# Retention: where the key-value products of a head pair are formed, summed and read

## The chip, the cores and the metric

The kernel runs on one core of a Trainium2 chip. The metric is the device time of one execution in microseconds. The engines are named as the profile names them: PE is TensorE (PEld its weight loads), DVE is VectorE, ACT is ScalarE, POOL is GpSimd, SP is SyncE, whose queue issues nearly all transfers.

## What is computed

Three stages follow each other, all in float32. First comes retention for 8 batches, 8 heads, 576 tokens and a head size of 64: causal attention without a softmax, where each score is damped by a power of the head's decay.

```python
scores = scale * np.matmul(q, k.transpose(0, 1, 3, 2))
gamma = 1.0 - 2.0 ** (-5.0 - np.arange(H, dtype=np.float32))
Dmat = np.where(rel >= 0, gamma[:, None, None] ** rel[None, :, :], 0.0)
return np.matmul(scores * Dmat[None], v)
```

Its output, 4608 tokens of 512 features, goes through `h = x @ w_in; (h * cos(h)) @ w_out` with 2048 hidden features, and that through a maximum of three projections to 768 features and a last product. The change is in the first stage.

## The kernel before

**Retention in chunks.** The 4608 tokens are taken in 9 blocks of 512 (`NB`). Sequences are 576 long, so most blocks hold the end of one sequence and the start of the next. `chunks_of` cuts a block at the sequence boundary and then into chunks of at most 128 tokens; blocks 1, 3, 5 and 7 get two chunks of 64. The token columns of a block are put in an order with the full chunks first and the two short ones together in the last 128 columns (`column_tokens`), and the host undoes that order at the end.

A unit of work is one block and one pair of heads (36 units, `att_unit`). Its load (`att_load`, line 560) brings query and key by feature, and key and value by token, 8,192 bytes per partition. GpSimd multiplies the values by the growth `gamma ** -pos`, a column of constants per unit (`att_scale`, 566). TensorE forms the scores of each chunk (`att_scores`, 578), VectorE masks them into SBUF (`att_mask`, 587). Each pair of heads has a running state of keys times values, 128x128 in a PSUM bank `state` that all pairs share and hold throughout; only the two diagonal 64x64 squares of it, one per head, are used. Chunk by chunk, ScalarE copies the state to SBUF for the chunk's later use and clears it where a sequence ends (`att_keep`, 605 and 607), and TensorE adds the chunk's product to it (`att_state`, 621). Then TensorE forms the outputs: each chunk's own part from the masked scores (`att_out`, 637, a head in each half of the array's columns) and the part from the kept state (649, two heads in opposite quarters). VectorE multiplies the result by the decay, chunk by chunk (`att_decay`, 664), into the input of the projections.

**The projections** use seven products of half-sized matrices in place of eight, each in three passes of a high and a low part of the operands. VectorE and GpSimd form the differences (386), ScalarE the high parts (390), VectorE the low parts (394). TensorE's products of the first projection during attention are line 417; line 439 is the later form for two blocks at a time. ScalarE and VectorE move sums out of PSUM (464, 470, 487), and `gate` computes `h * cos(h)` (521 to 534). Beside this, `background` prepares later weights: ScalarE widens (186, 187), VectorE joins (191, 192), GpSimd totals (198).

**What sets the order.** The kernel writes the order of every engine out by hand. `at(n, fn, turn)` puts work `n` slots ahead on an agenda with four turns, and `tick` at the end of a slot runs it. A slot after the lead is one product of the projections. Turn `INSIDE` is run in the middle of a slot's product, `AHEAD` at its end, `AFTER` and `LATER` behind that:

```python
at(start, lambda: att_scores(n), AHEAD)
for i in range(5):
    at(start + i + 1, lambda i=i: att_state(n, i), INSIDE)
at(start + 5, lambda: att_out(n), AHEAD)
at(start + 6, lambda: att_decay(n))
```

The first 8 units start 2 slots apart in a lead of 17 slots without projections, the others 3.75 slots apart on average (`start_of`). Each engine works through its queue in that order. PSUM has eight banks, given out in the order of the program (`bank`); SBUF tiles for units and weights come from a pool of eight (`w14`), for the rest from a pool of 25 (`x4`).

## Time and profile before

| | |
|---|---|
| Median of three runs | 1413.91 us (1413.03 to 1415.06) |
| Span of the profiled execution | 1410.5 us |
| Time of that execution outside its span | not recorded |
| PE busy | 1386.8 us, 98%, 8476 matmuls |
| DVE busy | 1130.2 us, 80% |
| ACT busy | 811.5 us, 58% |
| POOL busy | 189.6 us, 13% |

The profile is of one execution. "Busy" is time in which an engine has an instruction under way; a busy PE may still be waiting inside a pipeline. A group of instructions is named by its line, its engine, its output and its inputs. An idle time is put down to what ended it. The chain of waits follows the last instruction back, step by step, to what released it; a piece of the chain is the time for which that instruction held up what came after. An fp32 product is two passes (two records) on PE.

### The profile page before, as it was taken

Reading aid. Unit: us, or ns where it says so; the run is one execution under the profiler, and the core shown is the slowest. Engines: PE = TensorE matmul, PEld = TensorE weight load, DVE = VectorE, ACT = ScalarE, POOL = GpSimd, SP = SyncE. Lnnn points to the kernel's source line nnn. Section 1 sums busy time; section 2 is a strip of 40 time slices with the busy share of each in tenths; the row PEclk is TensorE's granted clock in tenths of the full one; section 3 lists DMA queues with packets and bytes.
Section 4 is the critical chain, followed back from the end, with each engine's and each line's share of the span. In section 5 each row is a group of like instructions: output and inputs, shape, how many; then the busy total and the mean of one; then the engine's idle time right before and its main releaser. Section 6 shows DMA issues by size and latency. Waiting matters only on the chain.

```text
span 1410.5 us, 22294 instructions
## 1 busy us (share of the span) xinstructions
PE 1386.8 (98%) x8476; PEld 1191.2 (84%) x8476; DVE 1130.2 (80%) x1532; ACT 811.5 (58%) x1322; POOL 189.6 (13%) x148
## 2 busy tenths in 40 slices
PE   7999999999999999999999999999999999999998
PEld 5899999998888887788888888889888888888887
DVE  7978888789677879989879999578678567868885
ACT  4566666567687676766546566444454344544543
POOL 3334443341011100000011110110010000000000
PEclk8999999999999999999999999999999999999999
DMA  9689988887989986475578987434434486345633
GB/s 367 236 291 315 312 313 308 293 323 253 412 307 376 337 292 239 185 269 194 175 247 228 296 238 224 124 125 167 172 112 142 147 323 234 102 157 165 230 105 119
DMA packets 112938, 333.36 MB, mean 236 GB/s; under 512 B 9920, under 2 KB 18112, under 8 KB 107200
## 3 DMA queue, kind: packets, MB, share of 16 engines
q1 hardware_dynamic: 109952, 322.51, 63.8%
q0 software_dynamic: 2880, 9.44, 3.8%
q8 instruction: 66, 1.08, 0.3%
q14 instruction: 40, 0.33, 0.1%
HBM read 194.02 MB, written 137.89 MB: 235 GB/s over the span
## 4 chain that ended last, share of the span: by engine, by line
PE 78%; DVE 4%; DMA 4%; ACT 1%; issue 1%; SPq 0%; POOL 0%; DVEq 0%; ACTq 0%
PE d_e L439 13%; PE d_g L928 11%; PE in L439 9%; PE b_e L439 6%; PE b_g L928 6%; PE d_a L417 5%; PE d_u L1458 5%; PE a_e L439 3%; PE a_g L928 3%; PE b_u L1458 2%; PE b_a L417 2%; PE d_b L417 2%; PE sc L578 1%; PE sums L417 1%; PE po L637 1%; PE a_u L1458 1%
## 5 line engine op out<-in xcount | busy, mean ns | idle before, releaser
L928 PE MATMUL d_g<-h_g,w_wo 128*128 128x512 f32 x512 | 157.9, 390 | 0.5 <-ACT o_g L951 0.5
L439 PE MATMUL in<-y,w_wi 128*128 128x512 f32 x672 | 153.6, 390 | 0.7 <-ACT s_a L1064 0.7
L439 PEld LDWEIGHTS in<-y,w_wi 128*128 128x128 f32 x672 | 125.8, 188 | 27.9 <-ACT s_a L1064 2.0
L895 DVE TENSOR_TENSOR l_g<-q_g,h_g 128x1024 fp32r<-128x1024 f32 x96 | 116.7, 1228 | 12.9 <-ACT h_g L888 9.3
L464 ACT ACTIVATE ext<-d_e 128x512 f32<-128x512 f32 x72 | 43.1, 599 | 144.9 <-PE d_e L439 144.9
L417 PE MATMUL d_a<-x_x,w_wi 128*128 128x256 f32 x864 | 122.8, 291 | 0.2 <-DVE x_x L394 0.2
L888 ACT CAST h_g<-q_g 128x1024 fp32r<-128x1024 f32 x96 | 98.9, 1051 | 32.2 <-DVE q_g L879 22.0
L417 PEld LDWEIGHTS d_a<-x_x,w_wi 128*128 128x128 f32 x864 | 109.0, 192 | 5.8 <-issue 1.7
L928 PEld LDWEIGHTS d_g<-h_g,w_wo 128*128 128x128 f32 x512 | 95.8, 188 | 20.6 <-ACT o_g L951 0.9
L928 PE MATMUL d_g<-l_g,w_wo 128*128 128x512 f32 x256 | 99.9, 390 | 0.2 <-DVE l_g L895 0.2
L525 DVE SCALAR_TENSOR_TENSOR t_a<-s_a,t_a 128x1024 f32<-128x1024 f32 x68 | 87.8, 1291 | 14.6 <-ACT t_a L521 13.8
L534 DVE SCALAR_TENSOR_TENSOR s_a<-t_a,s_a 128x1024 f32<-128x1024 f32 x68 | 89.9, 1322 | 10.0 <-ACT t_a L531 10.0
L605 ACT COPY u<-state 128x128 f32<-128x128 f32 x128 | 31.5, 266 | 94.7 <-PE state L621 94.2
L521 ACT ACTIVATE t_a<-s_a 128x1024 int32<-128x1024 f32 x68 | 72.0, 1059 | 21.6 <-DVE s_a L1067 15.3
L439 PE MATMUL d_e<-h_e,w_b 128*128 128x512 f32 x304 | 81.4, 390 | 0.1
L531 ACT ACTIVATE t_a<-t_a 128x1024 f32<-128x1024 f32 x68 | 72.0, 1058 | 13.6 <-DVE t_a L525 13.5
L928 PE MATMUL b_g<-h_g,w_wo 128*128 128x512 f32 x256 | 79.2, 390 | 0.4 <-ACT h_g L888 0.3
L468 DVE TENSOR_TENSOR ext<-ext,b_e 128x512 f32<-128x512 f32 x36 | 24.7, 686 | 59.7 <-PE b_e L439 52.0
L439 PEld LDWEIGHTS d_e<-h_e,w_b 128*128 128x128 f32 x304 | 56.9, 188 | 12.2 <-DVE ext L468 0.5
L417 PE MATMUL b_a<-x_x,w_wi 128*128 128x256 f32 x432 | 61.2, 289 | 1.2 <-DVE u L587 1.2
L566 POOL TENSOR_TENSOR u<-u,cs 128x512 f32<-128x512 f32 x36 | 46.5, 1294 | 81.4 <-DMA u<-att 72.1
L928 PEld LDWEIGHTS d_g<-l_g,w_wo 128*128 128x128 f32 x256 | 48.0, 188 | 11.0 <-DVE l_g L895 1.0
(367 smaller groups left out, 3373.7 us busy)
## 6 DMA issues: line engine op xcount, KB each, us to landing
u<-att SPq DMA_DIRECT2D x36, 1024.0 KB, 7.4
gqp<-s_a SPq DMA_DIRECT2D x64, 512.0 KB, 6.4
q_g<-gqp SPq DMA_DIRECT2D x64, 512.0 KB, 7.0
xsp<-x_x SPq DMA_DIRECT2D x56, 512.0 KB, 6.3
y<-xsp SPq DMA_DIRECT2D x56, 512.0 KB, 8.3
mqp<-ext SPq DMA_DIRECT2D x24, 512.0 KB, 3.6
st_b<-p_b SPq DMA_DIRECT2D x21, 512.0 KB, 6.4
w_b<-st_b SPq DMA_DIRECT2D x5, 1792.0 KB, 12.0
```

Source lines behind the costliest of these rows:

```text
L417: nc.tensor.matmul(h[:, p * HB : (p + 1) * HB], a, b, start=first and p == 0 and i == 0, stop=i == len(terms) - 1, skip_group_check=True,)
L439: nc.tensor.matmul(dst, a, b, start=first and i == 0, stop=i == len(terms) - 1, skip_group_check=True)
L464: nc.scalar.activation(dst, b[:, :n], AF.Copy, scale=scale)
L521: nc.scalar.activation(st["t"], s, AF.Copy, bias=0.25)
L525: nc.vector.scalar_tensor_tensor(out=r, in0=s, scalar=MOST_TURNS, in1=st["t"], op0=ALU.min, op1=ALU.subtract)
L531: nc.scalar.activation(r, r, AF.Sin, scale=TURN, bias=HALF_PI)
L534: nc.vector.scalar_tensor_tensor(out=s, in0=f32(st["t"]), scalar=-1.0, in1=s, op0=ALU.max, op1=ALU.mult)
L566: nc.gpsimd.tensor_tensor(out=v, in0=v, in1=cs[:, col : col + 8].unsqueeze(2).to_broadcast([128, 8, 64]), op=ALU.mult)
L888: nc.scalar.copy(h, ts[i][q])
L895: nc.vector.tensor_tensor(out=lo, in0=t, in1=f32(h), op=ALU.subtract)
L928: nc.tensor.matmul(to, a, v[:, p].rearrange("p (b n) -> p b n", b=2) if half and n == 2 else v[:, :, r], start=first and k == 0 and p == 0 ...
L1458: nc.tensor.matmul(dst, a, v, start=first and p == 0 and i == 0 and (wide or mt == 0), stop=p == 2 and i == 2, skip_group_check=True,)
```

## The change

The state bank, the copies of it and its clears go. Instead, each unit's keys times values are formed for each chunk and head by itself, 64x64, in a PSUM bank of their own, the two heads in the two halves of the array's columns (`att_products`). That is done in one go, right ahead of the outputs of the unit before (`att_visit`). ScalarE copies a unit's products out in one instruction, and GpSimd adds them up from chunk to chunk in SBUF (`att_states`); what crosses a block lies in `carry`, two places per pair in a tile that is not used otherwise at that time. Where a chunk of 64 ends a sequence, GpSimd clears its key rows, so that the product over all 128 rows is that of the other short chunk alone.

Queries and outputs keep their natural token order: the score product of two short chunks takes its query columns in two runs, the outputs of the short chunks are products of their own, and the decays are applied to 256 columns at a time, cut only where a sequence begins. The growth factors come with each unit's load, eight columns, and no longer with the constants, whose decay tables are 256 wide. The grouping of the rest of the kernel is not touched.

```diff
@@ -63,11 +63,11 @@
 CG = 0
-CM = CG + NPAIR * CH
+CM = CG + NPAIR * HB
 CM2 = CM + CH
 CGS = CM2 + CH
-CTV = CGS + NPAIR * 9
-NCONST = CTV + NBLK * NPAIR * 8
+NCONST = CGS + NPAIR * 9
+NTV = 8
 def constants():
@@ -76,18 +76,23 @@
     p = np.arange(128)
     for hp in range(NPAIR):
         g = gamma[2 * hp + p // 64]
-        c[:, CG + hp * CH : CG + (hp + 1) * CH] = g[:, None] ** np.arange(CH) / math.sqrt(D) / WSCALE
+        c[:, CG + hp * HB : CG + (hp + 1) * HB] = g[:, None] ** np.arange(HB) / math.sqrt(D) / WSCALE
         c[:, CGS + hp * 9 : CGS + (hp + 1) * 9] = g[:, None] ** (64 * np.arange(9))
     c[:, CM : CM + CH] = np.arange(CH)[None, :] >= p[:, None]
     c[:, CM2 : CM2 + CH] = c[:, CM : CM + CH] * ((np.arange(CH) // 64)[None, :] == (p // 64)[:, None])
+    return c.astype(np.float32)
+def growths():
+    gamma = (1.0 - 2.0 ** (-5.0 - np.arange(H, dtype=np.float32))).astype(np.float64)
+    tv = np.zeros((NBLK, NPAIR, 128, NB // CH, 2), np.float64)
     for j in range(NBLK):
-        pos = (column_tokens(j) % S).reshape(NB // CH, CH)
+        pos = (column_tokens(j) % S).reshape(NB // CH, CH).astype(np.float64)
         for hp in range(NPAIR):
-            for s in range(4):
-                for e in range(2):
-                    col = CTV + ((j * NPAIR + hp) * 4 + s) * 2 + e
-                    c[:, col] = gamma[2 * hp + e] ** (-pos[s].astype(np.float64))
-    return c.astype(np.float32)
+            for e in range(2):
+                tv[j, hp, :, :, e] = gamma[2 * hp + e] ** -pos.T
+    return tv.reshape(NBLK, NPAIR, 128, NTV).astype(np.float32)
@@ -553,29 +558,40 @@
         units[n] = {
             "qk": w[:, : 2 * NB].rearrange("p (a n) -> p a n", a=2),
             "kv": w[:, 2 * NB : 4 * NB].rearrange("p (a n) -> p a n", a=2),
-            "ret": w[:, 4 * NB : 6 * NB].rearrange("p (a n) -> p a n", a=2),
-            "um": w[:, 6 * NB :].rearrange("p (k n) -> p k n", n=CH),
-            "kept": {},
+            "tv": w[:, 4 * NB : 4 * NB + NTV],
+            "ret": w[:, 4 * NB + NTV : 6 * NB + NTV].rearrange("p (a n) -> p a n", a=2),
+            "sums": w[:, 6 * NB + NTV : 6 * NB + NTV + 4 * D].rearrange("p (k n) -> p k n", n=D),
+            "w": w,
         }
-        nc.sync.dma_start(out=w[:, : 4 * NB], in_=att[j, hp])
+        nc.sync.dma_start(out=w[:, : 4 * NB + NTV], in_=att[j, hp])
     def att_scale(n):
-        v = units[n]["kv"][:, 1].rearrange("p (s d) -> p s d", d=64)
-        col = CTV + n * 8
-        nc.gpsimd.tensor_tensor(
-            out=v, in0=v, in1=cs[:, col : col + 8].unsqueeze(2).to_broadcast([128, 8, 64]), op=ALU.mult
-        )
+        u = units[n]
+        v = u["kv"][:, 1].rearrange("p (s d) -> p s d", d=64)
+        nc.gpsimd.tensor_tensor(out=v, in0=v, in1=u["tv"].unsqueeze(2).to_broadcast([128, 8, 64]), op=ALU.mult)
+        for _, m, c, pos in chunks_of(order_of(n)[0]):
+            if m < CH and pos + m == S:
+                s, p = divmod(c, CH)
+                nc.gpsimd.memset(u["kv"][p : p + m, 0, s * CH : (s + 1) * CH], 0.0)
     def att_scores(n):
         u = units[n]
-        qT, kT = u["qk"][:, 0], u["qk"][:, 1]
+        ch = chunks_of(order_of(n)[0])
         u["sc"] = [bank(f"sc{n}_{e}") for e in range(2)]
         for s in range(NB // CH):
             sl = slice(s * CH, (s + 1) * CH)
+            runs = sorted((c, a) for a, _, c, _ in ch if c // CH == s)
             for e in range(2):
                 r = slice(64 * e, 64 * e + 64)
-                nc.tensor.matmul(u["sc"][e][:, sl], kT[r, sl], qT[r, sl], start=True, stop=True)
+                a = runs[0][1]
+                if len(runs) == 1:
+                    q = u["w"][r, a : a + CH]
+                else:
+                    apart = runs[1][1] - a
+                    q = u["w"][r, a : a + 2 * apart].rearrange("p (b d) -> p b d", b=2)[:, :, : CH // 2]
+                nc.tensor.matmul(u["sc"][e][:, sl], u["qk"][r, 1, sl], q, start=True, stop=True)
     def att_mask(n):
         u = units[n]
@@ -591,63 +607,71 @@
                         op=ALU.mult,
                     )
-    def att_keep(n, i):
...
+    def grown(n):
+        ch = chunks_of(order_of(n)[0])
+        return [i for i, (_, m, _, pos) in enumerate(ch) if pos + m < S]
+    def att_products(n):
+        u = units[n]
+        ch = chunks_of(order_of(n)[0])
+        kn, v = u["kv"][:, 0], u["kv"][:, 1]
+        u["kv_sums"] = b = bank(f"kv{n}")
+        for k, i in enumerate(grown(n)):
+            s = ch[i][2] // CH
+            for e in range(2):
+                cols = slice(s * CH + 64 * e, s * CH + 64 * e + 64)
+                nc.tensor.matmul(
+                    b[64 * e : 64 * e + 64, k * D : (k + 1) * D], kn[:, cols], v[:, cols], start=True, stop=True
+                )
+    def att_states(n):
         u = units[n]
         j, hp = order_of(n)
         ch = chunks_of(j)
-        if i >= len(ch):
-            return
-        _, m, _, pos = ch[i]
-        st = state[:, hp * CH : (hp + 1) * CH]
-        if pos:
-            um = u["kept"][i] = u["um"][:, len(u["kept"])]
-            nc.scalar.copy(um, st)
-        if pos + m == S:
-            nc.scalar.activation(st, cs[:, CM : CM + CH], AF.Copy, scale=0.0)
-    def att_state(n, i):
...
+        of = grown(n)
+        su = u["sums"]
+        nc.scalar.copy(su[:, : len(of)], u["kv_sums"][:, : len(of) * D].rearrange("p (k n) -> p k n", n=D))
+        before = carry[hp][(j + 1) % 2]
+        u["state"] = {}
+        for i, (_, m, _, pos) in enumerate(ch):
+            if pos:
+                u["state"][i] = before
+            if i not in of:
+                continue
+            k = of.index(i)
+            dst = carry[hp][j % 2] if i == len(ch) - 1 else su[:, k]
+            if pos:
+                nc.gpsimd.tensor_tensor(out=dst, in0=before, in1=su[:, k], op=ALU.add)
+            elif i == len(ch) - 1:
+                nc.gpsimd.tensor_copy(dst, su[:, k])
+            before = dst
+    def att_out(n):
         u = units[n]
         j, hp = order_of(n)
         ch = chunks_of(j)
-        if i >= len(ch):
-            return
-        kn, v = u["kv"][:, 0], u["kv"][:, 1]
-        _, m, c, pos = ch[i]
-        if pos + m < S:
-            s, p = divmod(c, CH)
-            sl = slice(s * CH, (s + 1) * CH)
-            nc.tensor.matmul(
-                state[:, hp * CH : (hp + 1) * CH],
-                kn[p : p + m, sl],
-                v[p : p + m, sl],
-                start=False,
-                stop=True,
-                skip_group_check=True,
-            )
-    def att_out(n):
...
         qT, v = u["qk"][:, 0], u["kv"][:, 1]
         po = u["po"] = bank(f"po{n}")
-        for s in range(NB // CH):
+        for i, (a, m, c, _) in enumerate(ch):
+            s = c // CH
             for e in range(2):
                 nc.tensor.matmul(
-                    po[64 * e : 64 * e + 64, s * CH : (s + 1) * CH],
+                    po[64 * e : 64 * e + 64, a : a + m],
                     v[:, s * CH + 64 * e : s * CH + 64 * e + 64],
-                    u["ret"][:, e, s * CH : (s + 1) * CH],
-                    start=s == 0,
+                    u["ret"][:, e, c : c + m],
+                    start=i == 0,
                     stop=False,
                     skip_group_check=True,
                 )
-        for i, um in u["kept"].items():
-            _, m, c, _ = chunks_of(j)[i]
+        for i, st in u["state"].items():
+            a, m, _, _ = ch[i]
             for e in range(2):
                 r = slice(64 * e, 64 * e + 64)
                 nc.tensor.matmul(
-                    po[r, c : c + m], um[r, r], qT[r, c : c + m], start=False, stop=True, skip_group_check=True
+                    po[r, a : a + m], st[r], qT[r, a : a + m], start=False, stop=True, skip_group_check=True
                 )
     def att_decay(n):
@@ -657,39 +681,44 @@
         half = f"k{hp // 2 + 1}"
         if half not in o:
             o[half] = x4(f"{half}_x{j}", [2, NB])
-        for _, m, c, pos in chunks_of(j):
-            t, cc = divmod(c, HB)
-            g = CGS + hp * 9 + pos // 64
+        cuts = sorted({0, HB, NB, (-j * NB) % S} & set(range(NB + 1)))
+        for lo, hi in zip(cuts, cuts[1:]):
+            t, cc = divmod(lo, HB)
+            g = CGS + hp * 9 + (j * NB + lo) % S // 64
             at_ = (hp % 2) * HB + cc
             nc.vector.scalar_tensor_tensor(
-                out=o[half][:, t, at_ : at_ + m],
-                in0=u["po"][:, c : c + m],
+                out=o[half][:, t, at_ : at_ + hi - lo],
+                in0=u["po"][:, lo:hi],
                 scalar=cs[:, g : g + 1],
-                in1=cs[:, CG + hp * CH : CG + hp * CH + m],
+                in1=cs[:, CG + hp * HB : CG + hp * HB + hi - lo],
                 op0=ALU.mult,
                 op1=ALU.mult,
             )
+    def att_visit(n):
+        if n + 1 < NUNIT:
+            att_products(n + 1)
+        att_out(n)
     def att_unit(n, start):
         at(max(0, start - 1), lambda: att_scale(n))
         at(start, lambda: att_scores(n), AHEAD)
-        at(start, lambda: att_keep(n, 0), AFTER)
         at(start + 1, lambda: att_mask(n))
-        for i in range(5):
-            at(start + i + 1, lambda i=i: att_state(n, i), INSIDE)
-            if i < 4:
-                at(start + i + 1, lambda i=i: att_keep(n, i + 1), AFTER)
-        at(start + 5, lambda: att_out(n), AHEAD)
+        if not n:
+            at(start + 1, lambda: att_products(n), AHEAD)
+            at(start + 1, lambda: att_states(n))
+        at(start + 5, lambda: att_visit(n), AHEAD)
+        if n + 1 < NUNIT:
+            at(start + 5, lambda: att_states(n + 1))
         at(start + 6, lambda: att_decay(n))
     NUNIT = NBLK * NPAIR
     nc.sync.dma_start(out=cs, in_=cst)
-    state = bank("state")
-    nc.tensor.matmul(state, cs[:, :CH], cs[:, :NB], start=True, stop=True, skip_group_check=True)
-    nc.vector.memset(state, 0.0)
+    carry = [[f32(spare)[:, (2 * hp + k) * D : (2 * hp + k + 1) * D] for k in range(2)] for hp in range(NPAIR)]
     sums_bank = bank("sums")
     nc.tensor.matmul(sums_bank, cs[:, :CH], cs[:, :NB], start=True, stop=True, skip_group_check=True)
     lead = {}
@@ -1568,9 +1597,7 @@
...
+        "att": np.concatenate([by_feature(q, slice(None)), by_feature(k, idx), by_token(k), by_token(v), growths()], axis=3),
```

The lines left out are the bodies of the old `att_keep`, `att_state` and `att_out`, which stand above, and the host's reordering.

## Rows read from the trace of the kernel before

**Rows 1.** Busy time by stretch: us; PE, PEld, DVE, ACT, POOL busy (instructions); PEclk, DMA share, GB/s.
```profile
20.00:66.30 46.30, 44.33 (x514) 37.97 (x513) 46.02 (x107) 26.90 (x71) 15.71 (x14) 0.99 0.74 265
66.30:320.00 253.70, 253.16 (x2562) 232.40 (x2561) 207.17 (x358) 160.50 (x321) 101.05 (x68) 1.00 0.87 308
320.00:338.40 18.40, 15.87 (x147) 15.20 (x146) 18.11 (x28) 11.83 (x21) 4.19 (x3) 1.00 0.48 174
```

**Rows 2.** Waits of PE, 44 to 330 us: us in total, times, longest.
```profile
PE b_a L417 <- DVE u L587: 1.2, 1, 1.2
PE state L621 <- ACT state L607: 0.8, 1, 0.8
```

**Rows 3.** Timeline of DVE and PEld near 62 us: start us, us, instruction.
```profile
62.30 0.69 DVE L394 TENSOR_TENSOR x_x<-tb_x,x_x 128x512 fp32r<-128x512 f32 x1
...
62.60 1.51 PEld L417 LDWEIGHTS d_a<-x_x,w_wi 128*128 128x128 f32 x12
```

**Rows 4.** The chain of waits after attention: start us, us, what.
```profile
361.76 122.44 PE in L439 x540
```

**Rows 5.** State products in the chain; lines 621 and 637, 66 to 330 us (durations ns).
```profile
286.84 0.41 PE state L621 x2
...
298.10 0.22 PE state L621 x2
...
L621 PEld LDWEIGHTS state<-u x184: 182/192/192, 67.7 to 321.7; 128*128 128x128 f32 x160, 64*128 64x128 f32 x24
...
L637 PEld LDWEIGHTS po<-u x432: 132/137/137, 72.5 to 325.6; 128*64 128x64 f32 x144
```

**Rows 6.** Output products in the chain: start us, us, passes.
```profile
171.79 0.80 PE po L649 x12
...
182.32 0.81 PE po L649 x16
...
289.29 0.92 PE po L649 x16
...
306.60 1.02 PE po L637 x16
307.63 1.02 PE po L649 x16
```

**Rows 7.** DVE reading PSUM: one timeline row; groups, 44 to 320 us (busy us, mean ns).
```profile
328.11 1.12 DVE L664 SCALAR_TENSOR_TENSOR k_x<-po,cs 128x128 f32<-128x128 f32 x4
...
L664 DVE SCALAR_TENSOR_TENSOR k_x<-po,cs 128x128 f32<-128x128 f32 x104 | 30.0, 340 | 6.7 <-PE po L649 6.6
...
L470 DVE SCALAR_TENSOR_TENSOR s_a<-b_a,s_a 128x512 f32<-128x512 f32 x15 | 10.3, 690 | 20.2 <-PE b_a L417 20.2
```

**Rows 8.** Timeline of POOL: a clear and a subtraction.
```profile
0.24 0.10 POOL L1582 MEMSET const-float32-0.0<- 128x1 f32 x1 [0.24 <-issue]
...
220.77 1.27 POOL L386 TENSOR_TENSOR tb_x<-k_x,ta_x 128x512 f32<-128x512 f32 x1
```

**Rows 9.** Timeline of DVE and POOL at 329 to 332 us.
```profile
329.15 0.41 DVE L205 TENSOR_TENSOR s_wi<-fa_wi 128x256 f32<-128x256 f32 x1
...
330.69 1.47 POOL L386 TENSOR_TENSOR ta_x<-k_x,k_x 128x512 f32<-128x512 f32 x1
...
330.93 1.51 DVE L207 TENSOR_TENSOR s_wi<-fa_wi 128x256 f32<-128x256 f32 x1
```

**Rows 10.** Timeline of PE at 164.7 us.
```profile
164.71 1.22 PE L417 MATMUL d_a<-x_x,w_wi 128*128 128x256 f32 x8 [0.25 <-DVE x_x L394]
```

**Rows 11.** Groups of ACT: busy us, mean ns, idle before and its releaser.
```profile
L605 ACT COPY u<-state 128x128 f32<-128x128 f32 x128 | 31.5, 266 | 94.7 <-PE state L621 94.2
...
L219 ACT ACTIVATE w_wi<-fa_wi 128x256 fp32r<-128x256 f32 x2 | 0.8, 417 | 0.3 <-POOL fa_wi L198 0.3
```

**Rows 12.** DMA issues: count, KB each, median us to landing.
```profile
u<-att SPq DMA_DIRECT2D x36, 1024.0 KB, 7.4
...
w_b<-st_b SPq DMA_DIRECT2D x5, 1792.0 KB, 12.0
```

More of the change, by code (lines that the diff above doesn't have):

```diff
@@ L613, in att_state @@
         ch = chunks_of(j)
-        if i >= len(ch):
-            return
-        kn, v = u["kv"][:, 0], u["kv"][:, 1]
-        _, m, c, pos = ch[i]
-        if pos + m < S:
-            s, p = divmod(c, CH)
-            sl = slice(s * CH, (s + 1) * CH)
-            nc.tensor.matmul(
-                state[:, hp * CH : (hp + 1) * CH],
-                kn[p : p + m, sl],
-                v[p : p + m, sl],
-                start=False,
-                stop=True,
-                skip_group_check=True,
-            )
-    def att_out(n):
-        u = units[n]
-        j, hp = order_of(n)
         qT, v = u["qk"][:, 0], u["kv"][:, 1]
         po = u["po"] = bank(f"po{n}")
-        for s in range(NB // CH):
+        for i, (a, m, c, _) in enumerate(ch):
+            s = c // CH
             for e in range(2):
                 nc.tensor.matmul(
-                    po[64 * e : 64 * e + 64, s * CH : (s + 1) * CH],
+                    po[64 * e : 64 * e + 64, a : a + m],
                     v[:, s * CH + 64 * e : s * CH + 64 * e + 64],
-                    u["ret"][:, e, s * CH : (s + 1) * CH],
-                    start=s == 0,
+                    u["ret"][:, e, c : c + m],
+                    start=i == 0,
                     stop=False,
@@ L1556, with by_feature @@
     idx = np.concatenate([column_tokens(j) for j in range(NBLK)])
-    def by_feature(a):
-        a = a.transpose(1, 3, 0, 2).reshape(NPAIR, 128, T)[:, :, idx]
+    def by_feature(a, order):
+        a = a.transpose(1, 3, 0, 2).reshape(NPAIR, 128, T)[:, :, order]
         return a.reshape(NPAIR, 128, NBLK, NB).transpose(2, 0, 1, 3)
@@ L1570 @@
     arrays = {
-        "att": np.stack([by_feature(q), by_feature(k), by_token(k), by_token(v)], axis=3).reshape(
-            NBLK, NPAIR, 128, 4 * NB
-        ),
+        "att": np.concatenate([by_feature(q, slice(None)), by_feature(k, idx), by_token(k), by_token(v), growths()], axis=3),
         "w_in": by_column(moe_w_in),
@@ L1593 @@
     got = got.reshape(NBLK, 128, 2, 2, 2, HB).transpose(0, 3, 5, 2, 4, 1).reshape(T, DM)
-    back = np.empty(T, np.int64)
-    back[idx] = np.arange(T)
-    return np.ascontiguousarray(got[back])
+    return np.ascontiguousarray(got)
```

## The prediction

> **What bounds the kernel now.** The page's busy table puts TensorE at 98% of the span. That is an average, so the view that I read next is busy time by stretch. Attention fills the first 326 us, and its stretches differ [rows 1]: from 20 to 66.3 us VectorE is busy 46.02 of 46.30 us; from 66.3 to 320 us TensorE 253.16 of 253.70 and VectorE 207.17; to 338.4 us VectorE again 18.11 of 18.40. The reader should see a TensorE that never stops between 66.3 and 320 us, with a VectorE that has 46.5 us to spare; before and after, VectorE sets the pace. The waits of TensorE say the same: from 44 to 330 us the two longest kinds are 1.2 and 0.8 us in all [rows 2]. Late in the early stretch TensorE is only a hair behind VectorE: the product whose weight loads start at 62.60 us takes a low operand that is being made from 62.30 to 62.99 us, and reads it from its fifth load of twelve on, some 0.5 us after the first [rows 3].
>
> From 362 us on nothing of the change is touched, and there the chain runs through TensorE for 122 us at a stretch [rows 4]. I let that part move as a block.
>
> **TensorE, the term that carries the forecast.** In the chain a state product of a full chunk costs 0.22 us, one of a 64-row chunk 0.41 us [rows 5]. After 66 us there are 184 records of line 621, two to an fp32 product: 92 products, of which 12 have 64 rows. They cost 80 x 0.22 + 12 x 0.41 = 22.5 us. The last two, up to 321.7 us, lie where VectorE is about to lead; without their 0.44 us, 22.1 us are on the path.
>
> The new products come in pairs, one per head, each 64 columns wide in output and in moving data, in two column halves. No row shows that form, so I price it from the carried-state outputs of line 649, whose two heads lie in opposite quarters of the array [rows 6]. A unit with three 128-token chunks (12 passes) takes 0.80 us, one with four (16 passes) 1.02: 0.055 us per pass. A unit with eight passes of 128 columns and eight of 64 takes 0.81: so eight passes of 64 cost what four of 128 do, plus 0.01, which is 0.029 each. A unit with twelve and four should then take 0.80 + 4 x 0.029 = 0.92, and does. The outputs of line 637, with all 128 rows and column halves as in the new products, also take 1.02 for 16 passes, so full rows are no dearer. Products for units 10 to 35 fall after 66 us: 90 chunks (3 in each of units 10 and 11, then 4, 3, 4, 3, 4, 3 in four units each), 360 passes. At 0.029 that is 10.4 us. The bounds are nothing (hidden in idle halves) and 0.055 us, the pass of 128 columns: 19.8 us. I take 0.029, since the 64-column pass is the nearest form. Net: 10.4 - 22.1 = **-11.7 us**.
>
> The other edits to TensorE are free. In the four blocks with 64-token chunks the outputs are split, eight passes of 64 columns for four of 128: +0.01 us a unit by the price above. Products and outputs share one visit and the column halves, so no change of array form is added to the one that line 637 enters now. The query columns in two runs have as many elements as before. State products of unit n+1 stand ahead of the outputs of unit n in TensorE's queue already, so the products bring these no new wait for a load.
>
> **VectorE.** The decay of a unit was four or five instructions and is now two or three. Four of 128 columns run in 1.12 us [rows 7]; each is 0.340 us long, so the next starts 0.26 after the last. Of 256 columns none is shown; between 0.340 (128) and 0.690 (512) a straight line gives 0.457. Two take 0.38 + 0.46 = 0.83, so 0.29 us a unit go; where the cuts leave three, 0.15 to 0.29: about 9 us over 36 units. That counts only where VectorE leads: seven units before 62 us (-2.0 us) and two after 320 us (**-0.6 us**). The middle has slack already.
>
> **GpSimd, and what it costs VectorE.** New there are 96 additions and 8 copies of 128x64 and 16 clears of 64x128. The nearest rows are a subtraction of 128x512 at 1.27 us and a clear of one column at 0.10 [rows 8]. One eighth of the difference, plus 0.10: an estimate of 0.25 us, bounds 0.10 and 1.27. GpSimd has room, at 101 of 253.7 us [rows 1]. But VectorE pays: a 128x256 addition takes 0.41 us alone and a subtraction of the same size 1.51 while GpSimd subtracts for 1.47 beside it [rows 9]. About half of VectorE's time goes to forms with both inputs in SBUF, so I charge half of 0.25 us per addition. Early: 24 additions, +3.0 us, less the 2.0 of the decays: **+1.0 us**, and TensorE's own saving is worth nothing there because VectorE leads. Bounds: -2.0 (no collision) and +4.0 (each one in full). Middle: 80 operations x 0.125 = 10 us more, less 6.5 by decays; VectorE goes from 207.2 to 211 us in a stretch of 242. It stays second, but at single points it delivers with nothing over, as at 164.71 us, where TensorE waits 0.25 us for a low operand [rows 10]. TensorE now comes to each such point some 0.5 us sooner. I charge three of seven blocks 0.5 us: **+1.5 us**, bounds 0 and 3.5.
>
> Here the rows and the Trainium skill meet. Its page "SBUF — State Buffer", section "Who interferes with whom", says that VectorE with two SBUF inputs and GpSimd reading SBUF shut each other out for a whole instruction. The 1.51 against 0.41 us agrees with a full block. By that rule each early addition would cost 0.25 and not 0.125 us, and the sum would be 3 us higher.
>
> **ScalarE.** 128 copies of 0.266 us go, and the 32 clears beside them; 36 copies of up to 128x256 come, at 0.417 by the nearest row [rows 11]. That frees over 19 us of an engine at 160 of 254 us and is worth nothing by itself. It waited 94 us for state products, but TensorE hardly waited for it [rows 2]. The new copy waits for the products of its visit, with that slot's evictions queued behind: one wait of the old kind where four were. The additions wait for the copy, and behind them on GpSimd stand the next unit's scaling and the weight totals. The sums are read at the next visit, 9.7 us later (27 visits between 72.5 and 325.6 us [rows 5]), and copy and three additions take 1.2 us; the cover is gone only if GpSimd is 8 us late.
>
> **DMA and the start.** The growth factors move from the constants to each load: 32 bytes more on 8,192 per partition, 0.4% of 7.4 us. Rows of 14,336 bytes take 12.0 us, less than in proportion, so a longer row costs nothing more [rows 12]. No DMA is added or moved on a queue. The constants grow by 224 columns, 115 KB at the early 265 GB/s [rows 1]: **+0.4 us** before everything else, bounds 0 and that. The state bank's clearing product goes, off the path, as the first scores wait for data anyway. PSUM: one bank was held by the state throughout; now each unit's products hold one for a moment. A visit wants two banks, for products and outputs, eight in use at most, as before.
>
> **Sum.** -11.7 - 0.6 + 1.0 + 1.5 + 0.4 = -9.4 us on a span of 1410.5. Of the profiled execution the span alone is given; the median of three runs, 1413.0 to 1415.1, is 3.4 us above it. Off the median: 1413.9 - 9.4 = **1404.5 us**. A change of 0.2%, 2.8 us, is about what a measurement here can tell from none.
>
> **Rivals.**
> *The early stretch gives too.* If the additions slip between VectorE's operations, the decays' 2.0 us stay and the 1.5 us are not lost: -11.7 - 0.6 - 2.0 + 0.4 = -13.9, 1400 us, and less with some of TensorE's early saving. For it: GpSimd is idle two thirds of the early stretch. Against: VectorE is not. Chance 0.15.
> *VectorE takes half.* Its 20.2 us of waits for TensorE before line 470 [rows 7] show that TensorE feeds it and it catches up in bursts. If every block's burst is tight, half of the 11.7 us is lost: 1410 us. Chance 0.13.
> *Slower, through GpSimd's additions.* Place: VectorE. Price: the whole addition. If one takes 0.5 us and every one collides, the early stretch grows by 24 x 0.5 - 2.0 = 10 us; in the middle VectorE rises by 40 - 6.5 to 241 us, level with TensorE's 242, and I count 4 us of waits there: -11.7 - 0.6 + 10 + 0.4 + 4 = +2.1, and more where the level load is uneven: 1417 us. It decides from about 0.45 us per addition. For it: the fixed cost of an addition is not shown. Against: 1.27 us for eight times the elements [rows 8]. Chance 0.08.
> *The halves do not overlap.* If the new pairs run one after the other, a pass costs 0.055 us: -2.3 in place of -11.7, in all 0.0: 1413.9 us, no change. Against: line 637's pairs. Chance 0.07.
>
> The forecast has 0.57, with a range of its own of 1399 to 1409. Faster: 0.56 of it, 0.15, and 0.09 of the half case: 0.80. Same: 0.01 + 0.03 + 0.06 = 0.10. Slower: 0.08 + 0.01 + 0.01 = 0.10. The range 1397 to 1412 leaves out the slower case, that of no change and the edges.
>
> **What would show it.** Right: passes of the products near 0.03 us in the chain, no wait of TensorE for a state copy, additions of about 0.25 us, line 664 (whatever its new number) under 0.9 us a unit, the second projection group still starting near 66 us, attention ending some 10 us sooner. Wrong: TensorE waiting for GpSimd's sums or VectorE's low operands by several us, additions of 0.5 us, product passes of 0.05.

## The result, and the profile after

The changed kernel takes 1398.5 us (median of four, 1397.2 to 1401.0) beside 1414.5 us for the kernel before on the same chip: a ratio of 0.9886, interval 0.9872 to 0.9901. The forecast was 1404.5 us, so the sign and the side were right, the time lies inside the range, and the gain was 16 us where 9.4 were forecast. The profiled execution of the changed kernel took 1398.66 us, its span 1396.9; the span before was 1410.5, so 13.6 us went inside the span, and it is these that the steps below account for. The medians are 2.4 us further apart than the spans: the median stands 4.0 us above the span of before's profiled execution, and 1.6 above that of the changed kernel's.

The page's head of the changed kernel (busy us, share of the span, instructions):

```profile
span 1396.9 us, 22865 instructions
...
PE 1365.9 (98%) x8794; PEld 1177.2 (84%) x8794; DVE 1127.0 (81%) x1467; ACT 789.8 (57%) x1198; POOL 234.2 (17%) x268
```

TensorE issues 318 matmul records more than before and is busy 21 us less. The same view by stretch as [rows 1], cut at the places that answer to 66.3, 320 and 338.4 us:

```profile
20.00:66.38 46.38, 41.18 (x603) 36.00 (x599) 46.10 (x88) 21.02 (x42) 28.60 (x41) 0.98 0.74 279
66.38:306.84 240.46, 239.76 (x2792) 222.55 (x2791) 206.18 (x318) 145.45 (x232) 131.91 (x158) 1.00 0.89 324
306.84:325.00 18.16, 15.69 (x144) 15.01 (x144) 18.11 (x26) 10.81 (x19) 4.30 (x3) 1.00 0.48 175
```

The pattern is the old one: VectorE full, TensorE full, VectorE full. Only the middle has shrunk. GpSimd went from 101 to 132 us there, VectorE from 207 to 206.

To compare kernels I use three marks. **A** is the start of the second group of projections; between A and **B** TensorE leads; B is the end of the last product in the chain of waits before VectorE takes over (in every run the same product); **C** is the start of the first product after TensorE's one long wait.

| kernel | median, us | ratio to before | A | A to B | B to C | span |
|---|---|---|---|---|---|---|
| before | 1414.5 | 1 | 66.30 | 253.9 | 18.1 | 1410.5 |
| changed | 1398.5 | 0.9886 (0.9872 to 0.9901) | 66.38 | 240.5 | 17.7 | 1396.9 |

From C to the end it is 1072.1 us before and 1072.4 after. So the change took 13.4 us out of the middle, 0.5 out of the tail, and put 0.1 on the start.

The chain of waits of the changed kernel (start us, us, what and how many passes), two visits that answer to [rows 5] and [rows 6]:

```profile
265.84 0.62 PE kv L625 x16
266.45 0.89 PE po L661 x20
267.34 0.92 PE po L673 x16
...
283.56 1.44 PE b_a L422 x12
285.00 0.50 PE kv L625 x12
285.50 0.88 PE po L661 x16
286.37 1.02 PE po L673 x16
287.39 3.06 PE d_a L422 x24
```

Products (line 625) and the outputs behind them (661) take 0.50 + 0.88 = 1.38 us for 12 product passes and 0.62 + 0.89 = 1.51 for 16; the outputs alone took 1.02 before. That is 0.030 us a pass; 0.029 was forecast.

The groups of the new instructions, 0 to 330 us (busy us, mean ns, then idle time before and its releaser), and for the first group of line 647 also its shortest, median and longest in ns:

```profile
L689 DVE SCALAR_TENSOR_TENSOR k_x<-po,cs 128x256 f32<-128x256 f32 (+3 forms) x96 | 34.2, 406 | 4.6 <-PE po L673 4.6
...
L647 POOL TENSOR_TENSOR u<-u 128x64 f32<-128x64 f32 x48 | 24.0, 501 | 15.6 <-ACT u L636 13.1
...
L647 POOL TENSOR_TENSOR u<-spare,u 128x64 f32<-128x64 f32 x24 | 11.2, 466 | 73.4 <-ACT u L636 73.4
...
L647 POOL TENSOR_TENSOR spare<-u 128x64 f32<-128x64 f32 x24 | 10.3, 427 | 1.3
...
L576 POOL MEMSET u<- 64x128 f32 x16 | 3.2, 198 | 0.0
L649 POOL COPY spare<-u 128x64 f32<-128x64 f32 x8 | 1.9, 236 | 0.0
```

```profile
L647 POOL TENSOR_TENSOR u<-u x48: 316/322/1342, 12.0 to 304.5; 128x64 f32<-128x64 f32 x48
```

The median addition takes 0.32 us, not 0.25, and single ones of that group up to 1.34; the mean over all 96 is 0.47. TensorE's waits in the middle (total us, times, longest), first of the kernel before, 66 to 320 us, then of the changed kernel, 66 to 305 us, come to 0.5 us in both, so the forecast hand-overs added nothing:

```profile
PE state L621 <- ACT u L605: 0.3, 1, 0.3
PE d_a L417 <- DVE x_x L394: 0.2, 1, 0.2
```

```profile
PE d_a L422 <- DVE x_x L399: 0.3, 1, 0.3
PE po L661 <- DVE k_x L689: 0.2, 1, 0.2
```

### The profile page after: what moved, and what is told of

It reads as the page before. It is cut to its first block, busy times and chain, and to the rows that moved or that the text cites. A ratio compares the mean times of both kernels' runs of the same rounds, so it can differ in the third digit from the quotient of the medians.

```text
span 1396.9 us, 22865 instructions
## 1 busy us (share of the span) xinstructions
PE 1365.9 (98%) x8794; PEld 1177.2 (84%) x8794; DVE 1127.0 (81%) x1467; ACT 789.8 (57%) x1198; POOL 234.2 (17%) x268
## 4 chain that ended last, share of the span: by engine, by line
PE 70%; DVE 5%; DMA 4%; ACT 1%; issue 1%; SPq 0%; POOL 0%; DVEq 0%; ACTq 0%
PE d_e L444 13%; PE d_g L957 11%; PE in L444 9%; PE b_e L444 6%; PE b_g L957 6%; PE d_u L1487 5%; PE a_e L444 3%; PE a_g L957 3%; PE b_u L1487 2%; PE d_a L422 2%; PE d_b L422 2%; PE a_u L1487 1%; PE b_b L422 1%; PE b_a L422 1%; DMA gqp<-s_a 1%
## 5 line engine op out<-in xcount | busy, mean ns | idle before, releaser
L422 PE MATMUL d_a<-x_x,w_wi 128*128 128x256 f32 x864 | 117.8, 289 | 1.3 <-DVE u L603 0.7
L957 PEld LDWEIGHTS b_g<-h_g,w_wo 128*128 128x128 f32 x256 | 47.9, 188 | 11.3 <-ACT h_g L917 1.6
L957 PEld LDWEIGHTS d_g<-l_g,w_wo 128*128 128x128 f32 x256 | 48.1, 188 | 10.8 <-DVE l_g L924 1.0
L422 PEld LDWEIGHTS b_a<-x_x,w_wi 128*128 128x128 f32 x432 | 54.1, 191 | 2.1 <-issue 0.3
```

What stands on the lines that cost most here:

```text
L422: nc.tensor.matmul(h[:, p * HB : (p + 1) * HB], a, b, start=first and p == 0 and i == 0, stop=i == len(terms) - 1, skip_group_check=True,)
L957: nc.tensor.matmul(to, a, v[:, p].rearrange("p (b n) -> p b n", b=2) if half and n == 2 else v[:, :, r], start=first and k == 0 and p == 0 ...
```

## The experiments

Ratios are to the kernel before on the same chip. Where the same kernel was run again, A, A to B and B to C repeated within 0.1, 0.5 and 0.1 us; what comes after C differed by several us from execution to execution (1072.4 and 1075.3). So causes are read from the marks, and the whole time only says whether it holds. B to C is left blank where no wait of 2 us or more by TensorE follows B, or where that wait stands elsewhere.

| kernel | median, us | ratio (interval) | A | A to B | B to C | span |
|---|---|---|---|---|---|---|
| no_adds | 1399.7 | 0.9895 (0.9882 to 0.9909) | 64.69 | 241.2 | 17.6 | 1398.8 |
| full_rows | 1407.9 | 0.9962 (0.9949 to 0.9975) | 68.09 | 250.1 | 18.1 | 1408.6 |
| full_width | 1407.7 | 0.9955 (0.9942 to 0.9968) | 67.36 | 249.9 | 17.7 | 1405.9 |
| decay_128 | 1400.9 | 0.9904 (0.9888 to 0.9919) | 67.15 | 241.6 | 18.1 | 1401.4 |
| after_again | 1400.9 | 0.9912 (0.9898 to 0.9926) | 66.44 | 240.9 | 17.6 | 1400.3 |
| adds_x3 | 1423.9 | 1.0079 (1.0066 to 1.0091) | 75.9 | 254.6 | | 1421.1 |
| apart | 1410.0 | 0.9979 (0.9970 to 0.9987) | 67.34 | 249.6 | | 1407.9 |
| late_split | 1396.8 | 0.9884 (0.9871 to 0.9898) | 66.48 | 240.7 | | 1394.1 |
| adds_dve | 1431.0 | 1.0129 (1.0106 to 1.0151) | 77.04 | 258.3 | | 1425.5 |
| prefix4 | 1398.5 | 0.9898 (0.9882 to 0.9915) | 65.35 | 240.9 | | 1399.6 |
| prefix8 | 1394.7 | 0.9875 (0.9860 to 0.9890) | 66.15 | 239.7 | | 1393.1 |

**full_rows: the kernel before, with the short chunks' state products over all 128 rows.** As in the change, GpSimd clears the key rows that don't belong.

```diff
+        for _, m, c, pos in chunks_of(order_of(n)[0]):
+            if m < CH and pos + m == S:
+                s, p = divmod(c, CH)
+                nc.gpsimd.memset(units[n]["kv"][p : p + m, 0, s * CH : (s + 1) * CH], 0.0)
...
-                kn[p : p + m, sl],
-                v[p : p + m, sl],
+                kn[:, sl],
+                v[:, sl],
```

> The kernel before, with one part of the change: GpSimd clears the key rows of a short chunk that ends a sequence, and the state product of the other short chunk runs over all 128 rows. Theory A: a 64-row product costs 0.41 us and another 0.19 us in the product that it interrupts, for the change of array form and back; with 128 rows it costs 0.22. Twelve lie between 66 and 320 us: 12 x 0.38 = 4.6 us less in that stretch, span 1406. Rival B: only the 0.41 goes down, 12 x 0.19 = 2.3 us, span 1408. Early stretch as before in both.

The middle lost 3.8 us. The same visit in the chain, before and then in full_rows:

```profile
285.81 1.03 PE b_a L417 x7
286.84 0.41 PE state L621 x2
287.26 0.79 PE b_a L417 x5
```

```profile
284.18 1.03 PE b_a L417 x7
285.21 0.22 PE state L625 x2
285.43 0.60 PE b_a L417 x5
```

The short product cost 0.19 us more itself, and 0.19 more in the five passes that came after it. I read this as TensorE changing its form for the 64 rows and changing back; I had charged the first half only. Twelve such products are 4.6 us at most; 3.8, or 0.32 each, came out. The start was 1.8 us later here. Most of it stands already at the third unit's scores, which begin at 18.38 us and before at 16.93, behind longer waits of TensorE for loads; why the loads came later is open, and only the middle is used.

**full_width: the changed kernel with the products of both heads in one, 128x128.** ScalarE then copies each head's square by itself.

```diff
-            for e in range(2):
-                cols = slice(s * CH + 64 * e, s * CH + 64 * e + 64)
-                nc.tensor.matmul(
-                    b[64 * e : 64 * e + 64, k * D : (k + 1) * D], kn[:, cols], v[:, cols], start=True, stop=True
-                )
+            cols = slice(s * CH, s * CH + CH)
+            nc.tensor.matmul(b[:, k * CH : (k + 1) * CH], kn[:, cols], v[:, cols], start=True, stop=True)
```

> The changed kernel with one 128-wide product per chunk for both heads, as the state product was, in place of two 64-wide ones; ScalarE copies the two squares in two instructions. Theory A: the two halves run beside each other, so a chunk costs 4 x 0.030 = 0.12 us now and 2 x 0.11 = 0.22 in the wide form; 90 chunks in the middle make 9 us more, span 1406. Rival B: the gain came from where the products stand and not from the halves; within 2 us of 1396.9. Early stretch unchanged in both.

The middle is 9.4 us longer than in the changed kernel, the start 1.0. Its chain:

```profile
294.46 0.67 PE kv L624 x6
295.13 1.02 PE po L663 x16
296.15 1.02 PE po L675 x16
```

Three products of two passes take 0.67 us, and the outputs behind them 1.02; the changed kernel takes 0.50 and 0.88 for the same. Over the 90 chunks of units 10 to 35: 90 x 0.223 = 20.1 us against 360 passes x 0.030 = 10.8, a difference of 9.3, which is what the middle shows. The column halves do run side by side. With full_rows' 3.8 us, 13.2 of the 13.4 us of the middle are accounted for. The 1.0 us at the start suggests that work of TensorE counts there too, a little; 0.4 of it stands already at the third unit's scores (17.98 us for 17.59), behind a wait for a load, and is not shown to be TensorE's work.

**apart: the changed kernel with a unit's products one slot later, alone between two projections.**

```diff
     def att_visit(n):
-        if n + 1 < NUNIT:
-            att_products(n + 1)
         att_out(n)
...
         if n + 1 < NUNIT:
-            at(start + 5, lambda: att_states(n + 1))
+            at(start + 6, lambda: att_products(n + 1), AHEAD)
+            at(start + 6, lambda: att_states(n + 1))
```

> The changed kernel with the products of the next unit one slot behind the outputs and no longer right ahead of them; the same work. Theory A: what a visit saves beside its halves is the change of array form and back, 0.38 us each time; about 26 more of them in the middle are 10 us, span 1407. Rival B: such a change costs only where the row count changes as for the 64-row products; span within 2 us of 1396.9.

The middle grew by 9.1 us, with 0.8 us of waits in it. The chain of apart:

```profile
296.82 1.63 PE d_a L422 x12
298.45 0.50 PE kv L625 x12
298.95 1.63 PE d_a L422 x12
300.57 1.09 PE sc L594 x16
301.67 1.63 PE b_a L422 x12
303.30 1.02 PE po L661 x16
```

The products take 0.50 us, as before, but the outputs 1.02 in place of 0.88, since they must now enter the column halves themselves; and the projection behind the products takes 1.63 in place of 1.44. That is 0.14 + 0.19 = 0.33 us a visit, and 27 visits make 8.9 of the 9.1 us. Placing the products ahead of the outputs is thus worth as much as splitting them: with either left out, the middle is 249.6 or 249.9 us. The Trainium skill, "TensorEngine Tiling (Array Packing)", section "Key Properties", says that a change of tiling mode drains TensorE; the trace agrees in that each such change lengthens the work behind it, by 0.14 to 0.19 us; a drain as such it does not show.

**no_adds: the changed kernel without GpSimd's additions and copies of sums.** The carried sums are zero instead; VectorE clears their tile at 0.93 us, when it has nothing else to do.

```diff
-            dst = carry[hp][j % 2] if i == len(ch) - 1 else su[:, k]
-            if pos:
-                nc.gpsimd.tensor_tensor(out=dst, in0=before, in1=su[:, k], op=ALU.add)
-            elif i == len(ch) - 1:
-                nc.gpsimd.tensor_copy(dst, su[:, k])
-            before = dst
+            before = su[:, k]
```

> The changed kernel without GpSimd's 96 additions and 8 copies; the chunks' products are used unsummed and the carried state is zero, so the output leaves out all sums. Theory A: early on VectorE leads, and the additions (24 there, 0.32 us each) shut it out. Then the second projection group starts 3 to 4 us before 66.4 us, the stretch from there to the hand-over at 306.8 us keeps its 240.5 us within 1, and the span falls by 3 to 4 us. Rival B: the additions cost nothing, since VectorE would be as late without them; start at 66.4, span within 1 us of 1396.9.

A comes 1.7 us sooner, so the 24 early additions cost 0.07 us each, not the 0.125 that I charged nor the whole 0.32. GpSimd did part of the waiting: in the changed kernel 23 of them, from 20 us to A, keep it busy 11.0 us, 0.48 each where the median is 0.32. The middle is no shorter: 80 operations there cost nothing.

**decay_128: the changed kernel with decays cut at 128 columns again.**

```diff
-        cuts = sorted({0, HB, NB, (-j * NB) % S} & set(range(NB + 1)))
+        cuts = sorted(({0, HB, NB, (-j * NB) % S} & set(range(NB + 1))) | {CH, 3 * CH})
```

> The changed kernel with the decays cut at 128 columns again, four or five instructions a unit. Theory A: VectorE sets the early stretch and the end of attention, so 0.29 us a unit come back there: start of the second group 2.0 us after 66.4, 0.6 us more from the hand-over on, nothing between; span 2.6 us up. Rival B: VectorE's work is not what sets the early stretch; span within 1 us of 1396.9.

The decays' groups of decay_128, 0 to 330 us (busy us, mean ns):

```profile
L689 DVE SCALAR_TENSOR_TENSOR k_x<-po,cs 128x128 f32<-128x128 f32 x128 | 36.7, 340 | 4.4 <-PE po L673 4.4
L689 DVE SCALAR_TENSOR_TENSOR k_x<-po,cs 128x64 f32<-128x64 f32 x32 | 7.4, 272 | 0.0
```

The two forms overlap: together VectorE is busy with them for 42.2 us, in place of 34.2. Of the 8.0 us (about 9 forecast), 1.8 lie before A and are felt as 0.8, 5.8 in the middle, felt as some 0.6 to 1.1, and 0.5 in the tail, felt in full.

**adds_x3: each addition done three times, the extra ones into columns that nothing reads.**

```diff
             if pos:
+                spot = 6 * NB + NTV + 4 * D
+                for _ in range(2):
+                    nc.gpsimd.tensor_tensor(out=u["w"][:, spot : spot + D], in0=before, in1=su[:, k], op=ALU.add)
                 nc.gpsimd.tensor_tensor(out=dst, in0=before, in1=su[:, k], op=ALU.add)
```

> The changed kernel with every addition on GpSimd done three times, twice into a corner of the unit's tile that nobody reads: 192 additions more, 0.32 us each, 61 us of GpSimd. Theory A, as the prediction had it: each early addition takes half its length from VectorE, which sets the early stretch: 48 x 0.16 = 7.7 us later start of the second group, and some of the middle; span 1405 or more. Rival B: GpSimd's short additions fall where VectorE needs nothing of them, or GpSimd does the waiting; span within 2 us of 1396.9.

With 0.96 us per addition in place of 0.32 the kernel is slower than before, by 0.8%: A 9.5 us later and the middle 14 us longer. Its waits of TensorE, 20 to 340 us, and busy time from 20 us to A:

```profile
PE kv L625 <- POOL u L572: 9.5, 8, 2.2
PE po L676 <- POOL u L650: 4.7, 5, 1.4
```

```profile
20.00:75.90 55.90, 45.30 (x604) 38.26 (x602) 48.90 (x93) 22.22 (x45) 46.41 (x87) 0.91 0.64 236
```

So the slower side of my forecast exists, but not where I put it. VectorE is idle for 7.0 of the 55.90 us, so it no longer sets the pace there (its busy time does grow, by 2.8 us there and by 10.8 in the middle). GpSimd is late itself, busy 46.41 of the 55.90 us. Its scaled values (line 572) stand in its queue behind the additions, and TensorE's next products wait for them. Of TensorE's waits in the middle, 6.5 us are these; 2.6 more go to one unit's load and 2.3 to VectorE.

**adds_dve: the additions and copies on VectorE.**

```diff
-                nc.gpsimd.tensor_tensor(out=dst, in0=before, in1=su[:, k], op=ALU.add)
+                nc.vector.tensor_tensor(out=dst, in0=before, in1=su[:, k], op=ALU.add)
             elif i == len(ch) - 1:
-                nc.gpsimd.tensor_copy(dst, su[:, k])
+                nc.vector.tensor_copy(dst, su[:, k])
```

> The changed kernel with its 96 additions and 8 copies of sums on VectorE in place of GpSimd. Theory A (the early 1.7 us are a price that GpSimd and its latency make; the middle has slack): the second projection group starts within 64.7 to 68 us, since 24 additions of about 0.15 us on VectorE come to 3 to 4 us where VectorE leads, less the 1.7 that GpSimd's cost; the middle stays 240.5 us to within 1 us. Rival (VectorE in the middle has less slack than its busy share says): the middle grows by 3 us or more, with TensorE waits for VectorE of that size.

The rival held, and more: the middle grew by 17.8 us and the start by 10.7, where I had expected at most 2 at the start. Four readings of adds_dve. The timeline of VectorE and GpSimd (start us, us) shows what an addition takes; the busy time by stretch, how full VectorE is; the waits of VectorE and TensorE, 20 to 345 us, what follows in the queues; the last two lines what TensorE does after a wait:

```profile
115.04 0.22 DVE L647 TENSOR_TENSOR u<-u 128x64 f32<-128x64 f32 x1
115.21 1.04 POOL L203 TENSOR_TENSOR ar_wi<-ar_wi 128x512 uint32<-128x512 uint32 x1 [12.75 <-DVE ar_wi L197]
115.30 1.04 DVE L647 TENSOR_TENSOR spare<-u 128x64 f32<-128x64 f32 x1
```

```profile
20.00:77.00 57.00, 47.14 (x598) 40.60 (x594) 56.09 (x116) 21.61 (x43) 17.99 (x19) 0.86 0.63 234
77.00:335.00 258.00, 245.45 (x2789) 226.63 (x2788) 234.62 (x389) 144.81 (x229) 101.19 (x80) 0.98 0.84 299
```

```profile
DVE u L647 <- ACT u L636: 16.1, 11, 4.3
...
PE d_a L422 <- DVE x_x L399: 10.3, 7, 2.8
PE sc L594 <- DVE u L603: 4.6, 4, 3.0
PE po L673 <- DVE u L647: 3.3, 5, 1.5
```

```profile
67.89 2.67 PE L594 MATMUL sc<-u 64*128 64x128 f32 x16 [2.95 <-DVE u L603]
...
67.00:71.00 4.00, 3.11 (x18) 2.78 (x19) 3.97 (x11) 0.23 (x1) 0.00 (x0) 0.50 0.79 254
```

An addition is shorter on VectorE, 0.22 us in the median, but takes 1.04 where GpSimd totals weights for 1.04 us beside it; in the middle the 70 additions recorded come to 36 us, some 0.5 each. That is load: VectorE is full in the early stretch, 56.09 of 57.00 us and no wait, and in the middle its busy time rises from 206 to 235 us. There it also waits 16 us in all for ScalarE's copy, at the head of its queue, with low operands behind it, for which TensorE waits 12 us. On GpSimd the same wait is 86 us long in all, and no wait of TensorE in the middle names GpSimd. How much of the 17.8 us the load makes and how much the queue was not separated. And a long idle stretch of TensorE costs twice: after the 2.95 us at 65 to 68 us the granted clock is 0.50, the lower level of 1.2 GHz, and score products that take 1.16 us elsewhere take 2.67; in the middle TensorE is busy some 6 us longer than in the changed kernel, for the same work. So the prediction's case in which VectorE takes TensorE's gain back exists; with the sums on GpSimd it did not come about.

**late_split: the changed kernel with three conversions of weights four, three and two slots later.**

```diff
-    for i, n in enumerate((-29, -22, -15, -8)):
+    for i, n in enumerate((-29, -18, -12, -6)):
```

> The changed kernel with three of the four conversions of later weights near attention's end 4, 3 and 2 slots later. Theory A: VectorE's load just before TensorE's 2.5 us wait at 322 us (three sums drawn out from 0.4 to 1.4 us by GpSimd beside them) is what that wait is made of; the wait goes, and with it the slower products behind it: 3 to 4 us off, span 1393.5. Rival B: the load only moves and TensorE waits for it some slots later; span within 1.5 us of 1396.9.

> The changed kernel once more, as the footing for the three runs beside it and to see how far the marks in the trace move between executions. Both theories: span 1396.9 within 2 us; second projection group at 66.4, hand-over at 306.8, first product after attention's end at 324.5, each within 1 us of the one before if the stretches are set by the order alone.

after_again is the changed kernel unaltered, on the same chip: its marks came out within 1 us as expected, its span 3.4 us above, where at most 2 were expected. TensorE's waits behind B, first in the changed kernel, then in late_split:

```profile
PE sums L422 <- ACT sums L492: 2.5, 1, 2.5
```

```profile
PE sums L422 <- ACT sums L492: 1.6, 1, 1.6
```

Each theory holds in part. The wait at 324.49 us is gone, and one of 1.6 us stands one `sums` later, at 334.23. The 24 passes of `d_a` that follow the old wait took 4.28 us, those that follow the new one take 2.88, at granted clocks of 0.61 (327 to 330 us) and 1.00 (334 to 337 us). The first product of the late form (line 444) starts at 343.53 us in the changed kernel and at 341.52 in late_split. The medians are 4.0 us apart, with intervals that just touch, so I call it a gain of about 2 us, the size that the marks show.

**prefix4 and prefix8: late_split with the sums of units 0 to 3, or 0 to 7, formed on TensorE.** The product for a chunk adds the chunks before it in the same place in PSUM, so these units have no additions, and 40 passes for 16. ScalarE copies the carried sum by itself. The limit shown is prefix8's; prefix4 has `NPAIR * 1`.

```diff
-        for k, i in enumerate(grown(n)):
...
+        of = grown(n)
+        for k, i in enumerate(of):
+            parts = of[: k + 1] if n < NPAIR * 2 else [i]
...
+                for x in parts:
+                    s = ch[x][2] // CH
...
+                        start=x == parts[0],
+                        stop=x == i,
```

> The kernel with the later conversions, and the running sums of units 0 to 3 formed on TensorE directly (a chunk's sum is the product of all chunks up to it, accumulated in PSUM), so that these units have no additions. Theory A (the early stretch is set by VectorE and by GpSimd's additions beside it, and TensorE has room): the second projection group starts 0.8 us before 66.4, about 65.6, span about 1393. Rival (TensorE's extra passes, 24 of 0.03 us at most in a unit, lie on the path early too): it starts at 66.4 to 68 us.

> The same for units 0 to 7. Theory A: the second projection group starts about 1.7 us before 66.4, near 64.7 as without any additions, span about 1392.4. Rival (TensorE's extra passes lie on the path): it starts at 66.4 us or later, later than with four units.

prefix4's A is 1.0 us sooner, as the first theory had it (0.8). prefix8's is sooner by 0.2 only, where 1.7 was expected. Busy time late in the early stretch, first of the changed kernel, then of prefix8:

```profile
44.00:66.00 22.00, 18.55 (x236) 16.64 (x236) 21.86 (x42) 12.14 (x25) 11.47 (x14) 1.00 0.49 170
```

```profile
44.00:66.00 22.00, 21.94 (x330) 20.36 (x327) 21.86 (x46) 12.89 (x27) 8.42 (x9) 1.00 0.62 217
```

TensorE has become as full as VectorE: its spare 3.5 us went into the extra passes. prefix8 is the fastest measured, 1394.7 us, but its interval overlaps those of the changed kernel and of late_split; what is sure of it is that the early gain is spent. prefix4's whole time shows no gain: its execution lost 6 us after 345 us, in a stretch that the edit doesn't touch.

## Why the prediction was right, and what it missed

**The pass price held.** 0.029 us a pass was read from line 649's mixed units; 0.030 was measured. Without the short chunks' extra, the forecast exchange is 92 x 0.22 - 0.44 - 10.4 = 9.4 us, and full_width shows 9.4. What I read as the price of a pass is in fact two things: the products pay 0.14 us to enter the column halves, and the outputs no longer do. The sum is the same only because the two stand together, as the step on TensorE's other edits said ("no change of array form is added").

**The short state products were undersized.** The step took 12 x 0.41 from the chain, 2.3 us above full ones. full_rows gives 3.8: the way back to the full form, 0.19 us, is paid by the projection pass behind, whose row I had not looked at. This is 1.5 us of the 4.2 inside the span that the forecast missed.

**The hand-overs did not come.** +1.5 us was charged to TensorE arriving sooner at VectorE's deliveries; the waits of the middle are 0.5 us, as before, and VectorE is busy 206 us where 211 were forecast. VectorE's slack of 34 us in 240 is spread well enough: even decay_128, with 5.8 us more of decays there, lost at most 1.1 us. With the 1.5 of the short products this makes 3.0 of the 3.2 us by which the middle (-10.2 forecast with the waits, -13.4 found) was off.

**The start: +1.4 forecast, +0.1 found, by terms that partly cancel.** Additions cost 1.7 us (3.0 charged), the longer decays gave 0.8 (2.0 charged). Halving the products gives up to 1.0 by full_width, which I had set to nothing because VectorE leads: [rows 3] already had TensorE only a hair behind, and prefix8 shows the same from the other side. The three come to -0.1 us, if they add; that the start stayed put is luck as much as working. Of the 0.4 us for the larger constants 0.3 can be seen: TensorE's first product waits for them until 4.71 us, and before until 4.38. Whether it reaches A is open, since one of the two first products is gone and the first scores start at 7.21 us where they started at 7.91.

**The tail** gave 0.5 us for 0.6. The decays take 0.95 us a unit, where the sign asked for under 0.9. **GpSimd's collisions:** the rule of the Trainium skill cited in the prediction, "SBUF — State Buffer", "Who interferes with whom", agrees with single rows (0.22 and 1.04 us in adds_dve), but neither the half that I charged per addition nor the whole came about in the sum (0.07 us of 0.32). Part of the waiting was GpSimd's, by the 0.48 us of an early addition; whether the rest met VectorE idle or in forms that read PSUM was not counted.

**The rivals.** The first rival, that the early stretch gives too, had the time nearest to the measured one, 1400 us, but its mechanism did not come: that stretch gave nothing (+0.1 us), and what the forecast lacked came from the middle. VectorE did not take half. The halves do overlap. The slower case needs additions three times as long, and then runs mainly through GpSimd's own lateness, not VectorE; from what length on it decides was not tried between 0.32 and 0.96 us.

## What to carry to other kernels

A small product in another array form costs its change of form twice, once in its own row and once in the next projection's; look at both rows, and place all work of one form side by side. A running sum belongs on an engine that has time for it and whose queue can stand still: a 0.22-us addition in a full engine's queue cost more here than the 0.32-us one on GpSimd, which was busy for 132 of 240 us; three times as much on GpSimd made it late in turn. Where two engines are level, relieving one by loading the other gains only as far as the other's spare time.

## What was not expected of the hardware

- A change of array form costs 0.19 us in the first full-array product after it (1.63 for 1.44 us) and 0.14 on the way into column halves (1.02 for 0.88).
- A 128x64 addition takes 0.32 us on GpSimd and 0.22 on VectorE in the median (0.47 and some 0.5 in the mean, beside each other's work); a copy of that size 0.24 and a 64x128 clear 0.20 on GpSimd. An eighth of the data of [rows 8] takes a quarter of the time.
- After 2.95 us without work TensorE's granted clock was 0.50 for the next 4 us, and 16 score passes took 2.67 us for 1.16.
